# A routed expert layer on one core: the search's counts divided anew between VectorE and ScalarE

## The chip, the core and the metric

The kernel runs on one core of one Trainium2 chip. The metric is the time of one execution on the device in microseconds (us). It is measured several times; the median is given. The profile belongs to one more execution of the same program.

The engines that matter here are TensorE (PE: matmuls; PEld: its weight loads), VectorE (DVE), ScalarE (ACT) and GpSimd (POOL). Each works through its own instructions in the order in which the program lists them, and waits on semaphores for the others. What stands behind a waiting instruction on the same engine waits too.

## The reference

Three layers follow each other. The input is x of shape 8 x 3072 x 256.

```python
X = fft(fft(x, axis=1), axis=2).real            # 24576 tokens x 256
h = X @ w_in;  g = elu(h);  y = g @ w_out       # 256 -> 2048 -> 256
logits = y @ w_gate                             # 24576 x 8 experts
order = argsort(-logits.flatten())              # all token-expert pairs, best first
for idx in order:                               # greedy, each expert takes at most N // E = 3072
    tok, e = idx // 8, idx % 8
    if assigned[tok] < 0 and counts[e] < cap: assigned[tok] = e; counts[e] += 1
for e in range(8):                              # each expert: relu MLP 256 -> 1024 -> 256 on its tokens
    out[mask_e] = relu(y[mask_e] @ w1[e]) @ w2[e]
```

## The kernel before, in words

`moe1` (the first 1990 us) computes the transform and the first MLP and leaves the rows y in DRAM and the logits L in SBUF. `moe2` does the routing and the eight experts. The change lies in `moe2` alone.

**Routing.** The greedy assignment is done as eight selections, `select(i)`. Each finds the next expert to be full and the value at which it is. The logits lie as sortable 32-bit keys, one half-word in `hm` (upper half, masked) and one in `kl`, with 128 partitions (16 tokens by 8 experts) of 1536 columns. `level` (line 280) searches one half of the key bit by bit, 16 levels from bit 15 to 0, and `select` calls it twice, first on `hm`, then on `vm`. So a selection has 32 levels, and seven selections after the first have 224. A level counts the keys that reach a candidate `cand`: ScalarE counts `NA` = 512 columns with a Sign activation and an accumulator (line 287, result `c2`), VectorE counts `ND` = 1024 columns with a compare and an accumulator (line 288, result `c1`). TensorE adds the counts over the partitions with two or three matmuls of 8 columns (`c1`, line 298; `c0` in the second search, line 300; `c2`, line 301). VectorE compares the sums with the capacity (line 303, flags in `jk`, largest flag in `ok`) and makes the next candidate (line 305). The flags of each level are added to `score` (lines 292 and 306), and after the 32 levels the expert with the largest score is taken (lines 328 on).

**Listing.** `listing(i)` turns the selection into a list of token numbers. For each of 12 chunks it makes one-hot blocks on VectorE: `oq` (lines 473, 474 and the scaling by the partition number `pcol` in line 476) and `oh` (line 481). One step later `place` multiplies them on TensorE (line 452, 16 matmuls). It also fetches the expert's weights and splits them into two parts (ScalarE, GpSimd). For i = 0 the scaling stands on ScalarE already (line 478), and GpSimd does line 474.

**Experts.** `expert(i)` works on 6 groups of 512 tokens. A group has two stages. In the first ("hps stage"), eight blocks f of six matmuls of 512 columns (line 555, tile `hps`, three buffers); after each block ScalarE makes `hh` (line 567) and VectorE makes `hl` (line 573), which frees the `hps` buffer. Then eight transposes (line 533) bring in the next group, with `yh` on ScalarE and `yl` on VectorE. In the second ("acc stage"), 32 steps of three matmuls of 256 columns (lines 596 to 598), and after each 16 of them ScalarE copies a result (`osb`, line 603).

**Who sets the order.** Selections and listings for later experts are woven into the matmuls of the present expert by a small planner that runs while the program is built. It keeps three model clocks (`ck.pe`, `ck.dve`, `ck.act`). `pe(c)` advances the first; `act(d)` and `dve(d)` put d behind the later of the engine's own clock and `ck.pe` + 200. A level charges `dve(DR)` with `DR` = 940 and `act(700)` and yields `after()`, the later of both clocks plus 80: the due time. Between the matmuls the expert yields; the planner then steps the listing, or else the selection, if its due time has passed on `ck.pe` and `ck.dve` is not more than a slack ahead. A step of the selection is allowed after every step of the acc stage (327 model units each), but in the hps stage only after the first matmul of a block f (217 units) and after its last (1302). Each `hh` charges `act(480)`, each `hl` `dve(610)`, each `osb` `act(500)`. The planner fixes the order only; on the chip TensorE waits at a level's matmul until the counts are there.

The first selection and the first listing come before any expert, with nothing beside them. The last ten groups (two-thirds of expert 6 and all of expert 7) run with all selections and listings done.

Of the kernel before, what the change touches and what calls it, by code (L numbers as in the profile page):

```python
# [11 lines left out]
BF16 = mybir.dt.bfloat16  # L12
I32 = mybir.dt.int32
U16 = mybir.dt.uint16
AF = mybir.ActivationFunctionType
OP = mybir.AluOpType
AX = mybir.AxisListType

B, S, D, F, E, FE = 8, 3072, 256, 2048, 8, 1024
# [142 lines left out]
def moe2(tc, yd, R, w1, w2, out):  # L162
    nc = tc.nc
# [4 lines left out]
    with ExitStack() as ctx:  # L168
        con = ctx.enter_context(tc.tile_pool(name="con2", bufs=1))
        ctx.enter_context(nc.allow_low_precision(reason="counts up to 2048 are exact in float16"))  # L170
        rt = ctx.enter_context(tc.tile_pool(name="rt", bufs=1))
# [6 lines left out]
        def rps(shape, dtype=F32):  # L178
            return psum.tile(shape, dtype, name="rps")

        pcol = con.tile([128, 1], F32, name="pcol")
# [12 lines left out]
        score = con.tile([128, E], F32, name="score")  # L194
# [25 lines left out]

        setup = consts()
        NT = NC * 128
        ND = 1024
        NA = NT - ND

        def small(name, w=1, dtype=F32, bufs=2):
            return rt.tile([128, w], dtype, name=name, bufs=bufs)
# [7 lines left out]
        now = [-1]  # L235
        draining = [False]
        WAIT = 10000
        SW, S1, S2, AF0, DR, PM, FR = 1000, 1300, 2000, 80, 940, 1, 2

        class Clock:  # L240
            pe = dve = act = ready = 0
# [6 lines left out]
        def act(d):  # L248
            ck.act = max(ck.act, ck.pe + 200) + d

        def dve(d, after=0):
            ck.dve = max(ck.dve, ck.pe + 200, after) + d
# [3 lines left out]
        def after():  # L256
            return max(ck.dve, ck.act) + AF0

        def select(i):
            if i:  # L260
# [8 lines left out]
                for hf in range(2):  # L269
# [7 lines left out]
                    dve(900)  # L277
                    yield after()

            def level(src, c0=None):  # L280
                cand = small("cand")
                nc.vector.memset(cand, 32767.5)
                thr = float(2 * CAP - 16 * (NA + (NT if c0 is not None else 0)))
                for k in range(15, -1, -1):
                    w = float(1 << k)
                    c1, c2, low = small("c1", 1, F16), small("c2", 1, F16), small("low")
                    nc.scalar.activation(junk2[:, 0:NA], src[:, ND:], AF.Sign, bias=cand, scale=-1.0, accum_out=c2)
                    nc.vector.tensor_scalar(junk[:, 0:ND], src[:, 0:ND], cand, None, op0=OP.is_ge, op1=OP.add,  # L288
                                            accum_out=c1)
                    nc.vector.tensor_scalar(low, cand, 0.5 - w if k == 0 else -w / 2, None, op0=OP.add)  # L290
                    if k < 15:
                        nc.vector.tensor_tensor(score, score, jk, op=OP.add)
                    next(setup, None)
                    dve(DR)
                    act(700)
                    yield after()
                    ps = rps([128, E])
                    nc.tensor.matmul(ps, c1.to_broadcast([128, 128]), es2, start=True, stop=False)
                    if c0 is not None:
                        nc.tensor.matmul(ps, c0.to_broadcast([128, 128]), esn, start=False, stop=False)  # L300
                    nc.tensor.matmul(ps, c2.to_broadcast([128, 128]), esn, start=False, stop=True)
                    ok, jk = small("ok"), small("jk", E)
                    nc.vector.tensor_scalar(jk, ps, thr, None, op0=OP.is_ge, op1=OP.max, accum_out=ok)
                    cand = small("cand")
                    nc.vector.scalar_tensor_tensor(cand, ok, w, low, op0=OP.mult, op1=OP.add)
                nc.vector.tensor_tensor(score, score, jk, op=OP.add)
                return cand

            nc.vector.memset(score, 0.0)
            hi = yield from level(hm)  # L310
            c0, hib = small("c0", 1, F16), small("hib")
            nc.vector.tensor_scalar(hib, hi, 0.5, None, op0=OP.add)
# [9 lines left out]
            nc.vector.tensor_scalar(gm, hm, hi, None, op0=OP.is_ge)  # L322
            dve(600)
            lo = yield from level(vm, c0)
            smx, sv, mn, sel = small("smx"), small("sv", E), small("mn"), small("sel", E)
            key, sgn, th, wix = (small(n, 1, I32) for n in ("key", "sgn", "th", "wix"))
            wb = rt.tile([128, 16], BF16, name="wb")
            nc.vector.tensor_reduce(smx, score, op=OP.max, axis=AX.X)
            nc.vector.tensor_copy(key, lo)
            nc.vector.scalar_tensor_tensor(sv, score, smx, em8, op0=OP.is_equal, op1=OP.mult)  # L330
# [82 lines left out]
        def listing(i):  # L413
# [35 lines left out]
            def place(c, oh, oq):  # L449
                pl = rps([128, 48]) if i else pl0  # L450
                for j in range(16):
                    nc.tensor.matmul(pl, oh[:, :, j], oq[:, :, j], start=j == 0 and (i > 0 or c == 0),  # L452
                                     stop=j == 15 and (i > 0 or c == NC - 1))
                if i == 0:
                    return
                if c:
                    nc.vector.tensor_tensor(pj, pl, pj, op=OP.add)
                else:
                    nc.vector.tensor_copy(pj, pl)

            for c in range(NC):
                js = slice(16 * c, 16 * c + 16)
                if i:
                    oh = rt.tile([128, 128, 16], BF16, name="oh", bufs=2)
                    oq = rt.tile([128, 48, 16], BF16, name="oq", bufs=2)
                else:
                    oh = ex.tile([128, 128, 16], BF16, name=("yh", "yl")[c % 2])
                    oq = ex.tile([128, 48, 16], BF16, name="h%s%d" % ("hl"[c % 2], c // 2), bufs=1)

                def row(a, n):  # L470
                    return a[:, js].unsqueeze(1).to_broadcast([128, n, 16])

                nc.vector.tensor_tensor(oq[:, 24:48], io16[:, 0:24], row(qb, 24), op=OP.is_equal)
                (nc.vector if i > 0 else nc.gpsimd).tensor_tensor(oq[:, 0:24], oq[:, 24:48], row(jb, 24), op=OP.mult)
                if i > 0:
                    nc.vector.tensor_scalar(oq[:, 24:48], oq[:, 24:48], pcol, None, op0=OP.mult)
                else:
                    nc.scalar.activation(oq[:, 24:48], oq[:, 24:48], AF.Copy, scale=pcol)
                dve(900)
                yield 0  # L480
                nc.vector.tensor_tensor(oh, io16, row(rb, 128), op=OP.is_equal)
                if prev:
                    place(*prev)
                prev = (c, oh, oq)
                dve(1300)
                if ck.pe > fetched + WAIT:
                    next(parts, None)
                yield after()
# [128 lines left out]
        class Stream:  # L617
# [9 lines left out]
            def step(self):  # L627
# [6 lines left out]
                return False  # L634

        sel_s = Stream(select, E)
        lst_s = Stream(listing, E)

        def ready(i):
# [655 lines left out]
```

## Time and profile before

| | us |
|---|---|
| median of 3 runs (3556.1 to 3559.21) | 3558.7 |
| the profiled execution | 3554.52 |
| its span, first to last instruction | 3552.7 |
| TensorE busy | 3348.4 (94%) |
| VectorE busy | 2784.1 (78%) |
| ScalarE busy | 2139.5 (60%) |
| GpSimd busy | 650.7 (18%) |
| mean granted clock of TensorE | 0.974 |

The busy share is an average over stages with different limits: until 1985 us TensorE is busy without a break, from 1997.3 to 2110 us it is nearly idle, then it shares its time between experts and routing, and from 3308.6 us on it has the experts alone. What a change of the routing is worth is read from the second and third stage.

### The profile page before, as it was taken

How to read it: one execution, taken by the hardware profiler on the slowest of the kernel's cores; microseconds unless marked ns; L12 is line 12 of the kernel's file. 1: busy time of each engine (PE TensorE's matmuls, PEld its weight loads, DVE VectorE, ACT ScalarE, POOL GpSimd, SP SyncE). 2: the span in 40 equal slices, each digit the busy share in tenths (PEclk: the TensorE clock that was granted, in tenths of full speed). 3: DMA queues.
4: the chain of work that ended last, by engine and by line, in shares of the span. 5: the costliest groups of instructions: out<-in, count | busy, mean ns of one | idle time of the engine just before them, and what ended most of it. 6: DMA issues, size and time to landing. Idle time of an engine off the chain costs nothing.

```text
span 3552.7 us, 62569 instructions
## 1 busy us (share of the span) xinstructions
PE 3348.4 (94%) x25464; PEld 3111.3 (88%) x25464; DVE 2784.1 (78%) x5264; ACT 2139.5 (60%) x2945; POOL 650.7 (18%) x836
## 2 busy tenths in 40 slices
PE   7999999999999999999999549999999999999998
PEld 4999999999999999999999437878788887888997
DVE  7888888888888888788778888787878788887332
ACT  4777777778777777787777534343434344343232
POOL 4000000000000000000000053333333342424232
PEclk9999999999999999999999759999999999999999
DMA  7112121121121211211100011111111011111110
GB/s 197 31 51 46 43 41 46 36 45 35 42 45 44 41 46 36 45 35 42 32 13 13 13 41 39 54 58 33 60 36 60 28 60 34 60 37 59 39 48 30
DMA packets 97080, 159.31 MB, mean 45 GB/s; under 512 B 18464, under 2 KB 68632, under 8 KB 94616
## 3 DMA queue, kind: packets, MB, share of 16 engines
q1 hardware_dynamic: 67016, 64.05, 7.5%
q0 software_dynamic: 24576, 80.21, 7.2%
q10 hardware_dynamic: 5200, 11.05, 1.0%
q8 instruction: 200, 3.28, 0.4%
q14 instruction: 88, 0.72, 0.1%
HBM read 91.78 MB, written 63.47 MB: 44 GB/s over the span
## 4 chain that ended last, share of the span: by engine, by line
PE 79%; DVE 17%; issue 1%; DMA 1%; ACT 0%; POOL 0%; SPq 0%; DVEq 0%; POOLq 0%; ACTq 0%
PE acc L1115 10%; PE acc L1114 10%; PE acc L1116 10%; PE hps L555 10%; DVE junk L288 7%; PE pq L1061 5%; PE pq L1063 5%; PE pq L1062 5%; PE acc L596 4%; PE acc L598 3%; PE acc L597 3%; PE rps L452 3%; PE pq L1065 3%; DVE hl L573 2%; PE pq L788 2%
## 5 line engine op out<-in xcount | busy, mean ns | idle before, releaser
L1116 PE MATMUL acc<-woh,gl 128*128 128x264 f32 x3072 | 872.8, 284 | 1.4 <-DVE gl L1101 1.4
L1115 PE MATMUL acc<-wol,gh 128*128 128x264 f32 x3072 | 874.1, 285 | 0.0
L1114 PE MATMUL acc<-woh,gh 128*128 128x264 f32 x3072 | 873.0, 284 | 1.0 <-DVE wol L1035 1.0
L1116 PEld LDWEIGHTS acc<-woh,gl 128*128 128x128 f32 x3072 | 578.0, 188 | 2.0 <-DVE gl L1101 1.9
L1114 PEld LDWEIGHTS acc<-woh,gh 128*128 128x128 f32 x3072 | 578.5, 188 | 1.2 <-issue 1.2
L1115 PEld LDWEIGHTS acc<-wol,gh 128*128 128x128 f32 x3072 | 577.6, 188 | 0.0
L1084 ACT ACTIVATE e<-h 128x1024 f32<-128x1024 f32 x384 | 407.8, 1062 | 158.9 <-DVE h L1078 158.9
L1077 DVE TENSOR_TENSOR h<-pq,qs 128x512 f32<-128x512 f32 x384 | 265.5, 691 | 283.3 <-ACT qs L1071 282.3
L1101 DVE TENSOR_TENSOR gl<-g,gh 128x1024 fp32r<-128x1024 f32 x384 | 468.5, 1220 | 1.5 <-ACT gh L1096 1.5
L1091 DVE SCALAR_TENSOR_TENSOR g<-e,h 128x1024 f32<-128x1024 f32 x384 | 467.3, 1217 | 0.1
L596 PE MATMUL acc<-w2h,hh 128*128 128x256 f32 x1536 | 453.3, 295 | 0.0
L598 PE MATMUL acc<-w2h,hl 128*128 128x256 f32 x1536 | 434.9, 283 | 7.5 <-DVE hl L573 7.5
L597 PE MATMUL acc<-w2l,hh 128*128 128x256 f32 x1536 | 435.2, 283 | 0.0
L573 DVE SCALAR_TENSOR_TENSOR hl<-hps,hh 128x512 fp32r<-128x512 f32 x384 | 259.3, 687 | 221.1 <-ACT hh L567 213.4
L1086 ACT ACTIVATE e<-e 128x1024 f32<-128x1024 f32 x384 | 407.3, 1061 | 10.7
L1096 ACT ACTIVATE gh<-g 128x1024 fp32r<-128x1024 f32 x384 | 403.7, 1051 | 2.1 <-PE acc L1115 2.1
L567 ACT ACTIVATE hh<-hps 128x512 fp32r<-128x512 f32 x384 | 227.9, 595 | 283.2 <-PE hps L555 238.4
L1071 ACT ACTIVATE qs<-pq 128x512 f32<-128x512 f32 x384 | 229.4, 597 | 208.7 <-PE pq L1065 204.2
L606 POOL DMA_INDIRECT out<-osb,yg x192 | 201.2, 1048 | 734.6 <-ACT osb L603 705.3
L555 PE MATMUL hps<-yh,w1h 128*128 128x512 f32 x768 | 311.1, 405 | 15.8 <-DVE hl L573 14.9
L555 PE MATMUL hps<-yh,w1l 128*128 128x512 f32 x768 | 309.4, 403 | 0.0
L555 PE MATMUL hps<-yl,w1h 128*128 128x512 f32 x768 | 304.9, 397 | 0.0
(320 smaller groups left out, 7525.4 us busy)
## 6 DMA issues: line engine op xcount, KB each, us to landing
yd<-ysb SPq DMA_DIRECT2D x48, 514.0 KB
zd<-zev SPq DMA_DIRECT2D x30, 385.5 KB
xa<-x SPq DMA_DIRECT2D x28, 384.0 KB
zt<-zd SPq DMA_DIRECT2D x16, 193.5 KB
xa<-w_out ACTq DMA_DIRECT2D x6, 512.0 KB
zt<-zd SPq DMA_DIRECT2D x32, 96.0 KB
yg<-yd,idx POOLq DMA_INDIRECT x192
out<-osb,yg POOLq DMA_INDIRECT x192
```

The costliest lines, as they stand in the source:

```text
L555: nc.tensor.matmul(ps, w[:, ws], v[:, c], start=c + k == 0, stop=c + k == 3)
L596: nc.tensor.matmul(acc[t // 2][:, t % 2], hh[:, ts], w2h[:, fs], start=f == 0, stop=False)
L597: nc.tensor.matmul(acc[t // 2][:, t % 2], hh[:, ts], w2l[:, fs], start=False, stop=False)
L598: nc.tensor.matmul(acc[t // 2][:, t % 2], hl[:, ts], w2h[:, fs], start=False, stop=f == 7)
L1084: nc.scalar.activation(e, st["h"], AF.Relu, scale=-1.0)
L1086: nc.scalar.activation(st["e"], st["e"], AF.Exp, scale=-1.0)
L1091: nc.vector.scalar_tensor_tensor(g, st["e"], -1.0, st["h"], op0=OP.add, op1=OP.max)
L1096: nc.scalar.activation(st["gh"], st["g"], AF.Copy)
L1101: nc.vector.tensor_tensor(st["gl"], st["g"], st["gh"], op=OP.subtract)
L1114: nc.tensor.matmul(o, st["gh"][:, i, ts], woh(c), start=c == 0, stop=False)
L1115: nc.tensor.matmul(o, st["gh"][:, i, ts], wol(c), start=False, stop=False)
L1116: nc.tensor.matmul(o, st["gl"][:, i, ts], woh(c), start=False, stop=c == 15)
```

## The change

- A level divides its 1536 columns differently: in selections 1 to 7 VectorE counts 640 and ScalarE 896 (before: 1024 and 512), in selection 0 VectorE counts 832 and ScalarE 704.
- The flags of a level are no longer added to `score` at once. Line 303 writes them into a slot of a new tile `hist` (128 x 32 x 8, bf16), and one reduction over the 32 slots gives `score` at the end of a selection. 30 additions in the loop, two behind it, and the clearing of `score` are gone.
- In listings 1 to 7 the scaling of the one-hot block by `pcol` stands on ScalarE, as it did for listing 0.
- The planner's charges are changed to go with it: a level charges `dve(750)` and `act(1000)`, the first half of a listing chunk `dve(750)` and `act(450)` (before: `dve(900)` alone).

```diff
-        ND = 1024
-        NA = NT - ND
...
-        SW, S1, S2, AF0, DR, PM, FR = 1000, 1300, 2000, 80, 940, 1, 2
+        SW, S1, S2, AF0, PM, FR = 1000, 1300, 2000, 80, 1, 2
...
+            ND = 640 if i else 832
+            NA = NT - ND
+            hist = rt.tile([128, 32, E], BF16, name="hist")
+
             def level(src, c0=None):
...
                     nc.vector.tensor_scalar(low, cand, 0.5 - w if k == 0 else -w / 2, None, op0=OP.add)
-                    if k < 15:
-                        nc.vector.tensor_tensor(score, score, jk, op=OP.add)
                     next(setup, None)
-                    dve(DR)
-                    act(700)
+                    dve(750)
+                    act(1000)
                     yield after()
...
-                    ok, jk = small("ok"), small("jk", E)
-                    nc.vector.tensor_scalar(jk, ps, thr, None, op0=OP.is_ge, op1=OP.max, accum_out=ok)
+                    ok = small("ok")
+                    nc.vector.tensor_scalar(hist[:, k + 16 * (c0 is not None)], ps, thr, None, op0=OP.is_ge,
+                                            op1=OP.max, accum_out=ok)
...
-                nc.vector.tensor_tensor(score, score, jk, op=OP.add)
                 return cand
 
-            nc.vector.memset(score, 0.0)
...
+            nc.vector.tensor_reduce(score, hist.rearrange("p k e -> p e k"), op=OP.add, axis=AX.X)
             nc.vector.tensor_reduce(smx, score, op=OP.max, axis=AX.X)
...
-                if i > 0:
-                    nc.vector.tensor_scalar(oq[:, 24:48], oq[:, 24:48], pcol, None, op0=OP.mult)
-                else:
-                    nc.scalar.activation(oq[:, 24:48], oq[:, 24:48], AF.Copy, scale=pcol)
-                dve(900)
+                nc.scalar.activation(oq[:, 24:48], oq[:, 24:48], AF.Copy, scale=pcol)
+                dve(750)
+                act(450)
                 yield 0
```

## Rows read from the trace of the kernel before

**Rows 1.** Page: span, busy time by engine, the chain's shares by line.
```profile
span 3552.7 us, 62569 instructions
...
PE 3348.4 (94%) x25464; PEld 3111.3 (88%) x25464; DVE 2784.1 (78%) x5264; ACT 2139.5 (60%) x2945; POOL 650.7 (18%) x836
...
PE acc L1115 10%; PE acc L1114 10%; PE acc L1116 10%; PE hps L555 10%; DVE junk L288 7%; PE pq L1061 5%; PE pq L1063 5%; PE pq L1062 5%; PE acc L596 4%; PE acc L598 3%; PE acc L597 3%; PE rps L452 3%; PE pq L1065 3%; DVE hl L573 2%; PE pq L788 2%
```

**Rows 2.** Busy time by window: length, then us (x instructions) per engine.
```profile
core 0: us, PE busy (x) PEld busy (x) DVE busy (x) ACT busy (x) POOL busy (x), PEclk, DMA share, GB/s
1997.30:2067.00 69.70, 7.32 (x80) 4.67 (x81) 60.96 (x249) 27.79 (x66) 0.00 (x0) 0.50 0.02 5
...
2150.20:2163.80 13.60, 12.39 (x59) 8.90 (x59) 12.38 (x41) 8.77 (x18) 6.28 (x8) 1.00 0.20 59
2163.80:2178.80 15.00, 14.06 (x124) 13.07 (x123) 13.32 (x47) 7.34 (x16) 2.17 (x4) 1.00 0.05 19
...
3331.70:3342.70 11.00, 11.00 (x51) 9.07 (x50) 4.84 (x7) 4.78 (x8) 4.95 (x7) 1.00 0.16 49
3342.70:3354.90 12.20, 12.20 (x105) 12.20 (x104) 1.92 (x2) 2.22 (x3) 3.12 (x6) 1.00 0.14 44
```

**Rows 3.** Weight loads by line, 2112 to 3308.6: busy, mean, idle before, releasers.
```profile
L598 PEld LDWEIGHTS acc<-w2h,hl 128*128 128x128 f32 x1216 | 232.9, 192 | 8.4 <-DVE hl L573 8.4
...
L555 PEld LDWEIGHTS hps<-yh,w1h 128*128 128x128 f32 x609 | 116.8, 192 | 42.6 <-DVE hl L573 20.5 <-issue 1.3
...
L298 PEld LDWEIGHTS <-c 128*128 128x128 f16 x224 | 21.5, 96 | 104.7 <-DVE junk L288 83.2 <-issue 14.1 <-DVE score L292 5.0
```

**Rows 4.** Durations by line (ns min/median/max, first and last start, shapes).
```profile
L288 DVE TENSOR_SCALAR_CACHE_REDUCE junk<-hm,cand x128: 1278/1279/1282, 1997.4 to 3172.8; 128x1024 bf16<-128x1024 uint16 x128
L287 ACT ACTIVATE junk<-hm,cand x128: 712/722/725, 1997.8 to 3172.8; 128x512 bf16<-128x512 uint16 x128
L313 ACT ACTIVATE junk<-hm,hib x8: 1575/1576/1577, 2031.4 to 3175.0; 128x1536 bf16<-128x1536 uint16 x8
L328 DVE TENSOR_REDUCE smx<-score x8: 161/161/161, 2067.3 to 3216.1; 128x1 f32<-128x8 f32 x8
L262 DVE TENSOR_REDUCE m<-L x7: 1737/1742/1747, 2109.8 to 3080.4; 128x192 f32<-128x1536 f32 x7
L476 DVE TENSOR_SCALAR oq<-oq,pcol x84: 319/321/3173, 2215.3 to 3298.4; 128x384 bf16<-128x384 bf16 x84
L478 ACT ACTIVATE hh<-hh,pcol x6: 614/616/617, 2075.8 to 2100.3; 128x384 bf16<-128x384 bf16 x6
```

**Rows 5.** Timeline of one level of the first selection (start us, us, engine, line).
```profile
2027.05 1.28 DVE L288 TENSOR_SCALAR_CACHE_REDUCE junk<-hm,cand 128x1024 bf16<-128x1024 uint16 x1
...
2028.39 0.10 PEld L298 LDWEIGHTS <-c 128*128 128x128 f16 x1 [1.94 <-DVE junk L288]
...
2028.41 0.12 PEld L301 LDWEIGHTS <-c 128*128 128x128 f16 x1
...
2028.65 0.17 DVE L303 TENSOR_SCALAR_CACHE_REDUCE jk<-rps 128x8 f32<-128x8 f32 x1 [0.17 <-PE rps L301]
...
2029.12 1.28 DVE L288 TENSOR_SCALAR_CACHE_REDUCE junk<-hm,cand 128x1024 bf16<-128x1024 uint16 x1
2029.21 0.72 ACT L287 ACTIVATE junk<-hm,cand 128x512 bf16<-128x512 uint16 x1 [1.26 <-DVE cand L305]
2029.83 0.19 ACT L287 ACTIVATION_READ_ACCUMULATOR junk<-hm,cand 128x1 f16 x1
```

**Rows 6.** Timeline: two successive levels in an acc stage, twelve matmuls between them.
```profile
2487.46 0.10 PEld L298 LDWEIGHTS <-c 128*128 128x128 f16 x1 [0.52 <-DVE junk L288]
...
2489.52 0.10 PEld L298 LDWEIGHTS <-c 128*128 128x128 f16 x1 [0.53 <-DVE junk L288]
```

**Rows 7.** Timeline of VectorE in an hps stage, between two counts.
```profile
2656.18 0.68 DVE L573 SCALAR_TENSOR_TENSOR hl<-hps,hh 128x512 fp32r<-128x512 f32 x1
2656.78 0.16 DVE L303 TENSOR_SCALAR_CACHE_REDUCE jk<-rps 128x8 f32<-128x8 f32 x1
```

## The prediction

> **What bounds the kernel now.** I began with the page. TensorE is busy for 94% of the span, yet the chain that ended last has the count on VectorE, line 288, among its larger lines with 7%, more than any single expert line of the second part but one [rows 1]. So there is a stage in which a count on VectorE sets the pace although VectorE is not the busiest engine.
>
> Then the windows [rows 2]. In the first selection (1997.3 to 2067 us) TensorE does 7.3 of 69.7 us, and VectorE is busy for 61: this stretch is nothing but levels, one behind the other. In the experts I set a group with a selection beside it against one without. Without, the hps stage takes 11.0 us and the acc stage 12.2, and TensorE has no gap. With a selection they take 13.6 and 15.0, together 5.4 us more. The group with a selection holds 183 TensorE instructions against 156; the 27 more are ten levels of two or three small matmuls.
>
> Third, what TensorE waits for from 2112 to 3308.6 us. Its weight loads in line 298, the first small matmul of a level, are preceded by 104.7 us of idle time over 224 levels, 0.47 each; the count on VectorE ends 83.2 of it. Waits for `hl` in lines 555 and 598 are 20.5 and 8.4 us [rows 3]. These 134 us are about what a faster routing can give back in the experts; the last ten groups have nothing to give.
>
> **The level, part by part.** Read one level of the first selection [rows 5]. VectorE's count starts at 2027.05, TensorE loads the sum of `c1` at 2028.39 (1.34 later) and that of `c2` at 2028.41 (1.36 later), the flags follow at 2028.65 and the next count at 2029.12. ScalarE starts 0.09 us after VectorE and its accumulator is read out 0.62 + 0.19 us later, so its count is there 0.90 us after VectorE's start. VectorE is last by 0.4 us: that is the slack which the new division spends.
>
> The prices. ScalarE takes 722 ns for 512 columns and 1576 for 1536, so 0.834 ns a column: 882 ns for 704, 1042 for 896 [rows 4]. For VectorE's count there is one width, 1279 ns for 1024. Its slope I bound by two rows: a VectorE reduction takes 161 ns for 8 elements and 1742 for 1536, 1.035 ns a column, and the count can't fall faster than in proportion, 1.249 ns. I take 1.035, since it comes from an instruction of the same engine that also runs through all columns and gives one number: 640 columns 0.40 us less (up to 0.48), 832 columns 0.20 us less (up to 0.24).
>
> *Selection 0* (832 and 704). VectorE's leg falls to 1.14 us. ScalarE's rises to 0.90 + 0.16 = 1.06, and some 0.06 to reach TensorE, the delay that stands between the end of VectorE's count and the load. The two are level, and a level gains 0.20 us: 32 x 0.20 = 6.4. The additions to `score` in the loop stand where VectorE waits for TensorE anyway (idle 0.17 before the flags [rows 5]): nothing. At the end two additions of about 0.1 fall away. The reduction of 256 elements costs 161 + 248 x 1.035 = 418 ns; its stride of eight elements is shown in no row, so between 0.4 and, at twice that, 0.8. Sum: 6.4 + 0.2 - 0.4 = 6.2 us, all on the path.
>
> *Selections 1 to 7* (640 and 896). VectorE's leg falls to 0.94, but ScalarE's rises to 0.90 + 0.32 = 1.22, with the hand-over 1.28 against the 1.36 at which `c2` was loaded. So of the 0.40 us only 0.08 come out of the loop; in the second search one more small matmul (line 300) moves ahead of the wait, for which I add up to 0.04. I take 0.10: the loop of 2.06 us between two successive levels of an acc stage [rows 6] becomes 1.96.
>
> That alone would be 22 us. The rest hangs on the planner's order, which I work out from its charges. In the **acc stage** a level was due 200 + 940 + 80 = 1220 units after it was placed, and is now due after 200 + 1000 + 80 = 1280. Steps of 327 let it in at 1308 in both cases: twelve matmuls between two levels, as in rows 6. They are worth 1.44 us (12.2 us less the transposes over 32 steps, 0.36 a step), the loop needs 2.06, the small matmuls 0.09, and the wait is 0.53. It becomes 0.43. Where an `osb` falls between, the new due time slips to five steps, and the wait nearly goes (0.07).
>
> In the **hps stage** ScalarE's clock carries `hh` as well. Before: 200 + 480 + 700 + 80 = 1460 units, and the next opening is at 1519, seven matmuls on. At 11.0 / 48 = 0.23 us these are worth 1.6 us, while the loop has an `hl` in it, behind which the flags stand on VectorE (0.60 us from the start of the one to the other [rows 7]). So TensorE waits here too. After: 200 + 480 + 1000 + 80 = 1760 misses that opening, and the next is at 2604: twelve matmuls or 2.75 us. The loop with an `hl` needs 1.96 + 0.60 = 2.56. The wait should go.
>
> Carrying the three clocks through one steady group I get four levels in the hps stage (after blocks 0, 2, 4 and 6) and seven in the acc stage (after steps 5, 10, 14, 18, 23, 27 and 31). That is eleven, so the selection does not fall behind (ten in the group of rows 2). Waits of a group: 4 x 0.43, 2 x 0.07, about 0.3 after step 5, where VectorE is still at `yl`, and 0.25 from step 31 to the end of block 0 (one step and six matmuls, 1.73 us): 2.4 us. 224 levels are 20.4 such groups: 49 us of waits in place of 104.7, **56 us** less. By the stages of rows 2: excess 5.4 us for ten levels now, 2.4 + 11 x 0.09 = 3.4 for eleven then, times 224 levels: 121 less 69, **52 us**. I take 50, a little under both, since the first levels of a selection meet the end of a listing and not a steady group.
>
> The seven reductions stand between the last level and the matmuls of line 342. If TensorE waits for each, they cost 7 x 0.42 = 2.9 us; I charge all of it.
>
> **The listing.** VectorE loses 84 instructions of 321 ns, 27 us; ScalarE takes them at 616 ns [rows 4], 52 us, beside 224 x 0.32 = 72 us of longer counts. GpSimd and the DMA queues issue what they did. The new wait is ScalarE's for line 474 on VectorE, and behind it on ScalarE stand `hh` and `osb`, for which `hl` and TensorE wait. From above: each scaling delays TensorE by its full 0.62 us, 52 lost. From below: all waits for `hl` in rows 3 go, 29 gained. I take 0: the block is used by TensorE one chunk later, and three `hps` buffers let `hh` come late by a block or two. If that cover is gone, it is the third rival below.
>
> **The sum.** 3554.5 (the profiled execution) - 6.2 - 50 + 2.9 = 3501.2. The median stands 4.2 above the profiled execution, so I forecast **3505**, and 3485 to 3525 if only the sizes are off.
>
> **The rivals.**
> 1. *Only the shorter loop.* The longer count lies in front of `hh` on ScalarE (0.32 us), `hl` follows late, and the wider spacing in the hps stage is used up by it. Then 22 + 6.2 - 2.9 = 25 us: 3533. For it: 2.75 against 2.56 is a thin margin. Against: ScalarE has room there, 8.8 busy of 13.6 us [rows 2].
> 2. *Hidden.* A wait taken from line 298 shows up at the next instruction of TensorE, and only the first selection gains: 3558.7 - 6.2 + 2.9 = 3555. Against it: in the groups without a selection TensorE has no gap at all.
> 3. *ScalarE becomes the bound, slower.* Scalings (52) and the longer counts in hps stages (four in eleven of 224, 81 x 0.32 = 26) hold `hh` by 78 us, against 53 gained: 3505 + 78 = 3583. It decides once two thirds of these holds reach TensorE, which needs `hh` to be late by more than the buffers bear, some 2.75 us. For it: VectorE is sometimes late by that much; one scaling took 3173 ns [rows 4]. Against: in the usual chunk 0.6 us stand against that cover.
> The Trainium skill ("ScalarE: Activation LUTs", section Rules for kernel authors) speaks for the third: multiplications belong on VectorE, not on ScalarE. The trace agrees on the price of one, 321 against 616 ns. By the rule the move costs 84 x 0.295 = 25 us (3530) wherever engine time is the bound; by the rows it is not, for ScalarE is idle for a third of such a stage now [rows 2].
> 4. *More.* Waits for `hl` go as well, since VectorE is freer: another 29 us, 3476.
>
> **How the numbers follow.** Forecast 0.62, the first rival 0.14, the second 0.06, the third 0.07, the fourth 0.11. For 8 in 10 the range takes in the first rival's and the fourth's centre and leaves out the second and third: 3474 to 3546. A measurement of this kernel can tell about 0.2% (7 us) from no change. Faster: 0.62 + 0.14 + 0.11 = 0.87; same 0.06; slower 0.07.
>
> **What would show it.** In the profile after: line 288 at about 0.88 us for 640 and 1.08 for 832 columns, line 287 at 1.04 and 0.88; a first selection of some 63.5 us; in the experts twelve hps matmuls between levels instead of six or seven, with no idle time in front of line 298 or 301 there; about 0.43 us in the acc stages, now in front of line 301, with ScalarE as releaser; the sum of both lines near 50 us. A hps stage with a selection near 11.6 us and an acc stage near 15. What would make the forecast wrong: waits of line 555 for `hl` well above 20 us, or ScalarE's `hh` waiting behind line 478.

## The result and the profile after

| | before | after |
|---|---|---|
| median, same chip, 4 runs each (us) | 3557.7 (3556.1 to 3559.2) | 3498.8 (3497.0 to 3501.2) |
| profiled execution | 3554.5 | 3501.2 |
| span | 3552.7 | 3499.4 |

The ratio is 0.984 [0.982, 0.985]: the change saves 59 us by the medians and 53.3 us between the two profiled executions. The forecast was 3505, and 3501.2 for the profiled execution. The total was met; several of its terms were not, and their errors cancelled.

Page after, to be read against [rows 1]: span, busy time by engine, shares of the chain that ended last.

```profile
span 3499.4 us, 62303 instructions
...
PE 3343.9 (96%) x25464; PEld 3121.6 (89%) x25464; DVE 2637.1 (75%) x4924; ACT 2253.9 (64%) x3029; POOL 649.7 (19%) x836
...
PE hps L553 14%; PE acc L1113 11%; PE acc L1112 11%; PE acc L1114 11%; PE pq L1059 5%; PE pq L1061 5%; PE pq L1060 5%; PE acc L594 4%; PE acc L595 4%; PE acc L596 4%; PE rps L452 3%; PE pq L1063 3%; ACT junk L289 3%; PE pq L786 2%; PE pq L865 1%
```

VectorE's count has left the chain, where it held 7%. ScalarE's count (line 289 now) stands in it with 3%: it is the new last leg of a level. TensorE's own lines took over the rest; `hps` alone rose from 10% to 14%.

Windows after, with the columns of [rows 2]: the first selection, then two groups with a selection beside them (hps stage, acc stage, hps stage, acc stage).

```profile
2000.00:2064.00 64.00, 7.35 (x80) 4.70 (x81) 53.16 (x218) 32.94 (x66) 0.00 (x0) 0.50 0.02 5
2147.40:2158.90 11.50, 11.50 (x58) 8.87 (x57) 9.85 (x32) 9.05 (x17) 5.84 (x7) 1.00 0.19 56
2158.90:2173.10 14.20, 13.86 (x120) 13.10 (x119) 10.63 (x41) 8.72 (x15) 2.30 (x6) 1.00 0.09 29
2173.10:2184.80 11.70, 11.70 (x63) 9.02 (x62) 9.74 (x31) 9.43 (x17) 5.96 (x8) 1.00 0.19 57
2184.80:2200.00 15.20, 14.64 (x127) 13.51 (x126) 10.47 (x44) 9.23 (x17) 2.18 (x4) 1.00 0.08 27
```

The first selection, from its first count to the maximum over the scores, shrank from 69.9 to 64.0 us. A hps stage takes 11.5 or 11.7 instead of 13.6 us, and in both TensorE is busy from end to end. The two acc stages take 14.2 and 15.2 us against 15.0, with five and seven levels in them against six: there some idle time is left (0.3 and 0.6 us here).

Weight loads after, 2105 to 3260 us, with the columns of [rows 3]: busy, mean, idle before, releasers.

```profile
L596 PEld LDWEIGHTS acc<-w2h,hl 128*128 128x128 f32 x1216 | 233.9, 192 | 0.2 <-DVE hl L571 0.2
...
L553 PEld LDWEIGHTS hps<-yh,w1h 128*128 128x128 f32 x624 | 118.8, 190 | 24.5 <-DVE hl L571 5.1
...
L531 PEld LDWEIGHTS tps<-identf,yg 128*128 128x128 f32 x317 | 38.3, 146 | 23.5 <-DMA yg<-yd,idx 18.3 <-issue 0.2
L301 PEld LDWEIGHTS <-c 128*128 128x128 f16 x224 | 21.9, 98 | 19.4 <-ACT junk L289 18.9
L298 PEld LDWEIGHTS <-c 128*128 128x128 f16 x224 | 21.7, 97 | 42.3 <-issue 17.3 <-DVE junk L290 7.8 <-DVE low L292 6.3
...
L342 PEld LDWEIGHTS <-gm 128*128 128x128 bf16 x84 | 3.0, 96 | 3.0 <-issue 2.7
```

The third and the last of these lines have counterparts in the kernel before that [rows 3] didn't hold (2105 to 3308.6 us):

```profile
L533 PEld LDWEIGHTS tps<-identf,yg 128*128 128x128 f32 x312 | 36.1, 144 | 11.5 <-DMA yg<-yd,idx 8.2 <-issue 0.2
...
L342 PEld LDWEIGHTS <-gm 128*128 128x128 bf16 x84 | 2.6, 96 | 1.2 <-issue 1.0
```

So the ledger of TensorE's waits in the experts reads: in front of a level's matmuls 104.7 -> 19.4 + 42.3 = 61.7 (-43.0); for `hl` 28.9 -> 5.3 (-23.6); for the token rows that the transposes need 8.2 -> 18.3 (+10.1). That is -56.5. VectorE spends 4.3 us on the seven reductions (0.61 us each), but TensorE waits only 1.8 us more for the matmuls of line 342 behind them (1.2 -> 3.0): -54.7. From the first to the last matmul of `hps` the experts took 1409.7 us before (2117.8 to 3527.5) and 1359.8 after (2114.4 to 3474.2): **-49.9**. The first expert matmul starts 3.4 us earlier: -6.0 from routing (5.9 of them in the first selection), +2.6 in the first 1990 us, whose code is unchanged. The tail is 25.2 us in both. -49.9 - 3.4 = -53.3, the difference of the spans.

### The profile page after: what moved, and what is told of

Its sections match the earlier page's. It is cut to its first block, busy times and chain, and to the rows that moved or that the text cites. A ratio compares the mean times of both kernels' runs of the same rounds, so it can differ in the third digit from the quotient of the medians.

```text
span 3499.4 us, 62303 instructions
## 1 busy us (share of the span) xinstructions
PE 3343.9 (96%) x25464; PEld 3121.6 (89%) x25464; DVE 2637.1 (75%) x4924; ACT 2253.9 (64%) x3029; POOL 649.7 (19%) x836
## 4 chain that ended last, share of the span: by engine, by line
PE 85%; DVE 6%; ACT 4%; issue 2%; DMA 1%; POOL 0%; another core or an unknown queue 0%; ACTq 0%; DVEq 0%; POOLq 0%
PE hps L553 14%; PE acc L1113 11%; PE acc L1112 11%; PE acc L1114 11%; PE pq L1059 5%; PE pq L1061 5%; PE pq L1060 5%; PE acc L594 4%; PE acc L595 4%; PE acc L596 4%; PE rps L452 3%; PE pq L1063 3%; ACT junk L289 3%; PE pq L786 2%; PE pq L865 1%
```

## What was tested

The theory that I took to the chip ("order"): the gain comes from the planner's new charges, which put twelve matmuls instead of six or seven between two levels of a hps stage; without them the shorter loop gives little. The rival ("work"): VectorE's shorter leg and fewer instructions give the gain by themselves, whatever the order.

All medians of one batch come from one chip and stand against the kernel before there (3543.3, 3547.2 and 3556.1 us). Waits are sums of TensorE's weight loads in the experts, in us; "length" is first to last `hps` matmul. `c_first_only` changes nothing in the experts, so it gives the values of the unchanged experts for its batch. Two executions of one kernel differ here: `b_old_charges` and `b_again` are one kernel, and so are `e_split832` and `e_again`, and their lengths are 5.0 and 11.8 us apart (last section). A few us between two rows say little unless the trace shows where they come from.

| kernel | batch | median | ratio [95%] | levels | `hl` | fetch | length |
|---|---|---|---|---|---|---|---|
| c_first_only | 1 | 3542.1 | 0.9993 [0.9982, 1.0004] | 100.6 | 26.6 | 2.6 | 1396.3 |
| a_charges_only | 1 | 3514.3 | 0.9912 [0.9894, 0.9929] | 74.8 | 11.6 | 19.1 | 1366.7 |
| b_old_charges | 1 | 3490.3 | 0.9847 [0.9830, 0.9865] | 62.2 | 11.2 | 2.5 | 1349.4 |
| d_scale_vector | 1 | 3493.9 | 0.9857 [0.9840, 0.9874] | 53.3 | 4.4 | 16.9 | 1352.8 |
| z_after (the change) | 2 | 3485.3 | 0.9822 [0.9805, 0.9840] | 53.1 | 5.4 | 14.5 | 1344.4 |
| b_again | 2 | 3492.8 | 0.9835 [0.9815, 0.9854] | 61.9 | 13.3 | 8.1 | 1354.4 |
| e_split832 | 2 | 3478.5 | 0.9801 [0.9784, 0.9818] | 51.8 | 5.7 | 12.5 | 1337.4 |
| h_act850 | 2 | 3489.4 | 0.9828 [0.9810, 0.9846] | 58.2 | 4.5 | 14.8 | 1350.0 |
| e_again | 3 | 3489.1 | 0.9811 [0.9792, 0.9830] | 60.3 | 5.7 | 14.2 | 1349.2 |
| k_early_lists | 3 | 3474.8 | 0.9770 [0.9752, 0.9787] | 59.3 | 8.4 | 4.4 | 1333.0 |
| j_old_split832 | 3 | 3497.6 | 0.9830 [0.9812, 0.9849] | 72.2 | 11.8 | 4.5 | 1361.2 |
| f_no_hist | 3 | 3497.4 | 0.9831 [0.9812, 0.9850] | 62.6 | 6.0 | 18.4 | 1356.4 |

### The order alone

```diff
 # kernel before, with only the new charges
-                    dve(DR)
-                    act(700)
+                    dve(750)
+                    act(1000)
...
-                dve(900)
+                dve(750)
+                act(450)
                 yield 0
```

> The kernel before with the planner's new charges alone (a level dve(750), act(1000); the first half of a listing chunk dve(750), act(450)); all the work stays as it was, 1024 columns on VectorE and 512 on ScalarE, the scaling on VectorE. Theory of the order (mine): most of the gain is the wider spacing of levels in the hps stages, which follows from the charges and not from the work. Then twelve hps matmuls (2.75 us) stand between levels, the loop with an hl in it needs 2.06 + 0.60 = 2.66, and the wait goes there; in the acc stages the wait stays at 0.53 per twelve matmuls. Waits in front of line 298 fall from 104.7 to some 65 us: 3518 us. Theory of the work (rival): VectorE's relief is what counts and the order follows it; then the time stays within 10 us of before, 3548 to 3560.

Measured: 29 us less, about half of the change's gain, where "order" wanted most of it. Weight loads of this kernel (2105 to 3300 us):

```profile
L556 PEld LDWEIGHTS hps<-yh,w1h 128*128 128x128 f32 x638 | 121.2, 190 | 25.9 <-DVE hl L574 6.2
L534 PEld LDWEIGHTS tps<-identf,yg 128*128 128x128 f32 x320 | 38.6, 146 | 24.0 <-DMA yg<-yd,idx 19.1 <-issue 0.2
L298 PEld LDWEIGHTS <-c 128*128 128x128 f16 x224 | 21.6, 96 | 74.6 <-DVE junk L288 55.1 <-DVE hl L574 14.1 <-issue 2.1
```

Spacing takes 26 us off the waits of line 298 and 15 off those for `hl`. With 1024 columns VectorE's count is still the last leg (55.1 us). The longer fetch wait is here too, with none of the work moved: it belongs to the order. The eight executions with the new charges have 12.5 to 19.1 us of it, the five with the old charges 2.5 to 8.2.

### The work alone

```diff
 # kernel after, with the old charges
-                    dve(750)
-                    act(1000)
+                    dve(940)
+                    act(700)
...
-                dve(750)
-                act(450)
+                dve(900)
                 yield 0
```

> The changed kernel with the old charges (a level dve(940), act(700); the first half of a chunk dve(900)): the work is moved, the order stays. Theory of the order: the first selection gains 6, the loop is 0.10 us shorter (22 us), and in the hps stages, where six or seven matmuls still stand between levels, a wait is left since hh comes behind the longer count on ScalarE: 3525 to 3535 us. Theory of the work: nearly the whole gain, 3495 to 3508 us.

> The kernel with the work moved and the old charges once more, now beside the changed one. Theory that spacing and work are two ways to one and the same gain: the two kernels differ by little, and what differs is the fetch of the next expert's rows (waits of the transposes: none here, 10 to 20 us there); then this one is 5 to 15 us faster than the changed kernel. Theory that the new charges add their own 29 us: this one is 20 us or more slower.

Measured: 53 us less without any wider spacing. "Order" wanted 3525 to 3535 and falls. Repeated beside the whole change (`z_after`) it came out 7.5 us above it, where I had now expected it below; the spreads of the two (3486.5 to 3495.7 and 3483.7 to 3487.9) just overlap. So the order adds little to the work, and no loss shows. The timeline of `b_again` shows why six matmuls are enough (VectorE and ScalarE in a hps stage):

```profile
2178.42 0.88 DVE L290 TENSOR_SCALAR_CACHE_REDUCE junk<-vm,cand 128x640 bf16<-128x640 uint16 x1
2178.48 1.04 ACT L289 ACTIVATE junk<-vm,cand 128x896 bf16<-128x896 uint16 x1
...
2179.29 0.68 DVE L570 SCALAR_TENSOR_TENSOR hl<-hps,hh 128x512 fp32r<-128x512 f32 x1
2179.43 0.19 ACT L289 ACTIVATION_READ_ACCUMULATOR junk<-vm,cand 128x1 f16 x1
...
2179.55 0.10 PEld L298 LDWEIGHTS <-c 128*128 128x128 f16 x1 [0.28 <-DVE low L292]
...
2179.89 0.17 DVE L303 TENSOR_SCALAR_CACHE_REDUCE hist<-rps 128x8 bf16<-128x8 f32 x1
...
2180.30 0.88 DVE L290 TENSOR_SCALAR_CACHE_REDUCE junk<-vm,cand 128x640 bf16<-128x640 uint16 x1
```

VectorE ends its 640 columns 0.9 us after it began and goes on to `hl`, while ScalarE still counts; when TensorE has both counts added, VectorE has nearly finished `hl`. The loop takes 1.88 us with an `hl` in it, and I had 1.96 + 0.60. In the kernel before, three counts of VectorE in a hps stage with an `hl` between each two:

```profile
2654.84 1.28 DVE L288 TENSOR_SCALAR_CACHE_REDUCE junk<-hm,cand 128x1024 bf16<-128x1024 uint16 x1
...
2657.17 1.28 DVE L288 TENSOR_SCALAR_CACHE_REDUCE junk<-hm,cand 128x1024 bf16<-128x1024 uint16 x1
...
2659.51 1.28 DVE L288 TENSOR_SCALAR_CACHE_REDUCE junk<-hm,cand 128x1024 bf16<-128x1024 uint16 x1
```

2.33 us. So the work takes 0.45 us off this level with an `hl`, and 0.09 off one without (below). It is so throughout: between two levels with seven `hps` matmuls (35 times) the median falls from 2.14 to 1.79 us, with six (20 times) from 2.34 to 1.81, with twelve matmuls of the acc stage (62 times) from 2.07 to 1.95. Summed up from `c_first_only` to `b_old_charges`, which have the same order, the intervals of six and seven give 27 of the 47 us that the experts gain, those of twelve 14.

### Is it the columns that hide `hl`?

```diff
 # j_old_split832: the work alone, divided less far
-            ND = 640 if i else 832
+            ND = 832
```

> The work moved and the old charges, with 832 columns on VectorE and 704 on ScalarE. In this order six or seven hps matmuls stand between levels. Theory that at 640 an hl is hidden there beside ScalarE's longer count: at 832 VectorE's count ends only when ScalarE's does, the hl comes behind it, and the intervals of six and seven matmuls grow from 1.9 to some 2.1, while those of twelve matmuls in the acc stage shrink from 1.96 to 1.87; the two cancel, within 5 us of b_again, 0.983 of before. Rival, that only the later of the two legs counts: intervals of 1.87 everywhere, 8 to 12 us faster than b_again, 0.980.

Measured 0.9830, level with `b_again`'s 0.9835, as the theory of the hidden `hl` has it. The two stand in different batches; the intervals show it more surely. With 832 columns two levels of the acc stage with twelve matmuls between them come quicker (median 1.86 us instead of 1.95), those of a hps stage slower: 1.89 instead of 1.79 with seven matmuls between them and 2.06 instead of 1.81 with six, where the rival had 1.87 everywhere. Line 298 waits for VectorE again (2105 to 3300 us), first here, then in `b_again`:

```profile
L301 PEld LDWEIGHTS <-c 128*128 128x128 f16 x224 | 21.9, 98 | 0.0
L298 PEld LDWEIGHTS <-c 128*128 128x128 f16 x224 | 21.5, 96 | 72.2 <-DVE low L292 28.1 <-DVE junk L290 24.9 <-issue 10.7
```

```profile
L301 PEld LDWEIGHTS <-c 128*128 128x128 f16 x224 | 21.6, 97 | 22.2 <-ACT junk L289 19.0
L298 PEld LDWEIGHTS <-c 128*128 128x128 f16 x224 | 21.5, 96 | 39.7 <-DVE low L292 17.5 <-issue 11.5 <-DVE junk L290 1.4
```

### The even division with the new order

```diff
 # e_split832 and e_again: the change, but
-            ND = 640 if i else 832
+            ND = 832
```

> The changed kernel with 832 columns on VectorE and 704 on ScalarE in all selections, charges as changed. Both legs of a level are then about level (1.14 and 1.12) and the loop 1.87 in place of 1.96. If the loop is all that the acc stages wait for: 75 intervals of twelve matmuls by 0.09 less, 7 us faster than the changed kernel. If VectorE's relief counts (0.20 us more work of VectorE in 224 levels, an hl no longer fits beside ScalarE's count): 5 to 20 us slower than it.

> The changed kernel with 832 and 704 columns in all selections, once more, beside the next three on one chip: 0.980 of before. The transposes wait some 10 us for the fetched rows.

Measured 6.8 us less than the change on the same chip, with no overlap of the runs: the size that was expected, but not for the reason given. The 75 intervals of twelve matmuls in the acc stages, which were to give it, take 139.0 us in `z_after` and 139.9 in `e_split832`. The waits of line 301 for ScalarE are gone (20.0 to 0.3 us), but those of line 298 rise from 33.1 to 51.5. What gets shorter is the way from an acc stage into a hps stage: the 14 intervals of three acc and six `hps` matmuls take 26.5 us in place of 30.4. Where the order gives a level twelve matmuls in the hps stage, `hl` no longer needs hiding there, and the even division does a little better. `e_again` gave 0.9811 in the next batch, where its old-charge twin `j_old_split832` was 8.5 us slower, again without overlap. So the new charges are worth some 8 us on top of the work (7.5 and 8.5 side by side), not 29: **the two halves of the change are two ways to the same waits.**

### The list that comes late

With the new charges the transposes for expert 2 stand still. Timeline after, TensorE's loads and GpSimd's fetches:

```profile
2458.23 0.97 POOL L522 DMA_INDIRECT yg<-yd,idx  x1 [14.99 <-issue]
...
2461.01 0.29 PEld L531 LDWEIGHTS tps<-identf,yg 128*128 128x128 f32 x2 [4.40 <-DMA yg<-yd,idx]
2462.32 0.29 PEld L531 LDWEIGHTS tps<-identf,yg 128*128 128x128 f32 x2 [1.02 <-DMA yg<-yd,idx]
2464.78 0.72 PEld L531 LDWEIGHTS tps<-identf,yg 128*128 128x128 f32 x4 [2.17 <-DMA yg<-yd,idx]
```

The fetches are issued 3 us ahead of their use, 1.25 us apart; in the kernel before, the like fetches begin at 2460.94 and their transposes at 2477.51, 16.6 us later. The selections have become longer, measured in TensorE's matmuls: selections 1 and 2 took 2.7 and 2.5 groups (48 `hps` and 96 acc matmuls each) from first level to last, and take 3.0 and 3.0 now. The second, whose list expert 2 needs, ends 104 matmuls (0.7 of a group) later. The clock falls with it:

```profile
2456.00:2481.20 25.20, 17.77 (x128) 15.54 (x127) 9.81 (x42) 8.33 (x14) 9.87 (x13) 0.80 0.19 53
```

The granted clock of this stretch is 0.80 in the mean: part of it ran at 1.2 and not at 2.4 GHz. In steps of 5 us from 2455 on the clock is 0.76, 0.50, 0.72, 1.00 and 1.00, so it fell during the 7.6 us of waits for rows and rose behind them. Two kernels ask what would bring the list earlier: a smaller charge on ScalarE's clock, or the old order for the first two selections in the experts.

```diff
 # h_act850: the change, but
-                    act(1000)
+                    act(850)
```

> The changed kernel with a level charged act(850) in place of act(1000). The due time in the hps stage, 1610, still misses the opening at 1519, so twelve matmuls stay between levels there; in the acc stages it slips to five steps less often, so a selection takes fewer groups and the next list is ready earlier. Theory that the longer due time delays the list: the waits of the transposes fall from 10 to 20 us to below 5, while the acc stages wait a little more; 5 to 12 us faster than the changed kernel. Rival, that these waits come from the listing's own charges: no change, within 4 us.

Missed: 3489.4 against 3485.3, too near to tell apart, and the fetch wait stands at 14.8 us. In selections 1 and 2, on which the first lists depend, a level comes at the same place as with 1000 or one step of the acc stage earlier: in the hps stage both due times, 1610 and 1760, fall between the same two openings, 1519 and 2604.

```diff
 # k_early_lists: the even division, and the old order for selections 1 and 2
-            ND = 640 if i else 832
+            ND = 640 if i in (1, 2) else 832
...
-                    dve(750)
-                    act(1000)
+                    dve(940 if i in (1, 2) else 750)
+                    act(700 if i in (1, 2) else 1000)
```

> As e_again, but selections 1 and 2 with the old level charges (940, 700) and 640 columns on VectorE, selections 3 to 7 with the new charges and 832. Theory that the wait for the fetched rows comes from the first lists, which the new charges end a quarter of a group later: the waits of the transposes fall from 10 us to below 2, the granted clock stays up there, and the kernel is 6 to 12 us faster than e_again. Rival, that they come from the listing's charges, which stay as in e_again: no change, within 4 us.

Measured 14.3 us less than `e_again` beside it, more than expected, and the lowest ratio of all: 0.977 [0.975, 0.979]. Weight loads, 2105 to 3300 us, and the window 2430 to 2480 us, of `e_again`:

```profile
L531 PEld LDWEIGHTS tps<-identf,yg 128*128 128x128 f32 x326 | 38.5, 143 | 19.3 <-DMA yg<-yd,idx 14.2
```

```profile
2430.00:2480.00 50.00, 42.94 (x289) 36.85 (x288) 27.86 (x80) 18.72 (x36) 14.78 (x19) 0.90 0.12 35
```

and the same of `k_early_lists`:

```profile
L531 PEld LDWEIGHTS tps<-identf,yg 128*128 128x128 f32 x334 | 39.5, 144 | 9.0 <-DMA yg<-yd,idx 4.4 <-issue 0.2
```

```profile
2430.00:2480.00 50.00, 46.72 (x317) 40.27 (x316) 36.04 (x116) 27.11 (x52) 17.79 (x24) 0.97 0.14 44
```

The fetch wait falls by 9.8 us and the clock stays up: the wait does come from the late list. But the 14.3 us are not the price of that list. Counted from the first matmul of expert 0, expert 2 begins only 3.5 us earlier than in `e_again`, since the old order had put the kernel 6.0 us behind before the fetch. And `e_again` loses 8.7 us in experts 2 and 3 at two levels with long waits that `e_split832`, the same kernel, does not have (last section). Against `e_split832` the experts of `k_early_lists` are 4.4 us shorter. That early lists are worth more than this is not shown.

### The smaller parts

```diff
 # c_first_only: kernel before, but
-        ND = 1024
+            ND = 1024 if i else 832
```

> The kernel before with 832 columns on VectorE and 704 on ScalarE in selection 0 alone. The first selection is 32 x 0.20 = 6.4 us shorter, nothing else moves: 3551 us. If ScalarE's leg were the later one by more than I think, half of it: 3554.

The time can't tell it (0.9993, with 1 inside the interval). By the trace the first selection takes 63.6 us for 69.9 in the kernel before, measured from the first count to the maximum over the scores: -6.3, where 32 x 0.20 = 6.4 was forecast for the division alone.

```diff
 # d_scale_vector: the change, but the scaling of listings 1 to 7 on VectorE with its old charges
-                nc.scalar.activation(oq[:, 24:48], oq[:, 24:48], AF.Copy, scale=pcol)
-                dve(750)
-                act(450)
+                if i > 0:
+                    nc.vector.tensor_scalar(oq[:, 24:48], oq[:, 24:48], pcol, None, op0=OP.mult)
...
+                dve(900)
```

> The changed kernel with the scaling of listings 1 to 7 back on VectorE and its charge dve(900) without act(450). My forecast gave the move nothing: 3499 us, within 5. If the waits for hl that fell from 28.9 to 5.3 us between the two traces fell because VectorE is rid of 84 scalings, they come back here: 3510 to 3522. If ScalarE's waits at line 475 (126 us in all) hold TensorE, it is faster here: below 3490.

0.9857, against 0.984 and 0.9822 for the change in the result and in batch 2; with the first the intervals overlap, with the second they touch. If the move to ScalarE is worth anything it is a gain of up to some 12 us (0.35% of 3547), and not the loss that a price of 616 for 321 ns suggests. The waits for `hl` do not come back (4.4 us), so it is not the move of the scaling that took them away. Which wait it takes away I can't show: the waits of this kernel differ from the change's by less than two executions of one program do.

```diff
 # f_no_hist: the change, but the flags are added in the loop again
+                    if k < 15:
+                        nc.vector.tensor_tensor(score, score, jk, op=OP.add)
...
-            nc.vector.tensor_reduce(score, hist.rearrange("p k e -> p e k"), op=OP.add, axis=AX.X)
```

> The changed kernel with the flags added to score in every level, as before, and without the reduction. If the additions lie where VectorE waits anyway and the reduction (0.608 us, eight times) lies on the path: 5 us faster than the changed kernel. If in the hps stages the addition stands in front of an hl or the flags: 224 x 0.08 at most, 18 us slower, and the reduction given back, some 5 us: between 5 us faster and 13 slower; near 0.982 of before if both cancel.

0.9831, against 0.984 and 0.9822 for the change: no difference that can be told. TensorE's wait in front of the matmuls behind the selection is 1.2 us again, as before the change. Summing the flags once is neither a gain nor a loss of a size that shows. That the additions stood in VectorE's waiting time fits this; no run shows it by itself.

> The changed kernel itself, beside the next three on one chip. Both theories: 0.984 of before. Its waits: some 57 us in front of the level's matmuls, some 5 for hl, some 10 to 20 in front of the transposes for the fetch of the next expert's rows.

The change in batch 2: 0.982, at the lower end of the result's interval.

## Why the prediction came out, point by point

**Prices: right.** Durations after (ns min/median/max, starts, shapes), to be read against [rows 4]:

```profile
L290 DVE TENSOR_SCALAR_CACHE_REDUCE junk<-hm,cand x128: 878/879/1080, 2000.0 to 3158.3; 128x640 bf16<-128x640 uint16 x112, 128x832 bf16<-128x832 uint16 x16
...
L289 ACT ACTIVATE junk<-hm,cand x128: 882/1042/1045, 2000.3 to 3158.4; 128x896 bf16<-128x896 uint16 x112, 128x704 bf16<-128x704 uint16 x16
...
L327 DVE TENSOR_REDUCE score<-hist x8: 595/608/620, 2063.3 to 3204.8; 128x8 f32<-128x256 bf16 x8
...
L475 ACT ACTIVATE oq<-oq,pcol x84: 604/617/621, 2219.1 to 3271.6; 128x384 bf16<-128x384 bf16 x84
```

879 and 1080 ns were forecast as 0.88 and 1.08 us, 1042 and 882 as 1.04 and 0.88: a slope borrowed from another instruction of the engine held. The reduction was mis-sized: 608 ns instead of 418, within the bounds (0.4 to 0.8), so seven take 4.3 instead of 2.9 us on VectorE; TensorE's waits for them grew by 1.8 us.

**First selection: right.** 64.0 us against some 63.5; by the same marks 5.9 us less than before, where 6.2 was forecast.

**The loop of an acc stage: right in size.** Two successive levels after, with [rows 6] as their counterpart:

```profile
2170.05 0.10 PEld L298 LDWEIGHTS <-c 128*128 128x128 f16 x1
...
2170.37 0.10 PEld L301 LDWEIGHTS <-c 128*128 128x128 f16 x1 [0.21 <-ACT junk L289]
...
2172.34 0.10 PEld L301 LDWEIGHTS <-c 128*128 128x128 f16 x1 [0.21 <-ACT junk L289]
```

1.97 us from one to the next, forecast 1.96, and ScalarE is the releaser; the median of 75 such intervals is 1.94. The gap booked in front of line 301 is 0.21, not 0.43, because TensorE already does the matmuls of `c1` and `c0` in that time; twelve matmuls of 0.12 us still leave some 0.4 us beyond the levels' own matmuls.

**The order: right.** Two levels of a hps stage after, twelve matmuls apart, with nothing but an issue gap in front of each:

```profile
2174.57 0.10 PEld L298 LDWEIGHTS <-c 128*128 128x128 f16 x1 [0.27 <-issue]
...
2177.49 0.10 PEld L298 LDWEIGHTS <-c 128*128 128x128 f16 x1 [0.26 <-issue]
```

2.92 us, which is also the median of 55 such intervals. From 2174 to 2200 us the four levels of the hps stage and the seven of the acc stage stand where the clocks carried through put them.

**The reason given for the gain: half wrong.** The failed step is "The loop with an `hl` needs 1.96 + 0.60". `hl` runs beside ScalarE's longer count, and a loop with it takes 1.88 us in `b_again`. Even in the kernel before, it added 2.33 - 2.06 = 0.27 and not 0.60. The 0.60 ran from the start of `hl` to the flags, but without an `hl` the flags wait for TensorE at that place: 0.26 us from the load to the flags in [rows 5]. The sum counted that time twice. From the 0.60 it followed that without the wider spacing only the first rival's 25 us would be left; the work alone gave 53.

**Waits for `hl`: the size was off.** I left them at 28.9 us; they fell to 5.3, and that is the mechanism of the fourth rival (its 3476 was not reached). Each half of the change does it: 11.6 with the order alone, 11.2 with the work alone.

**"The selection does not fall behind": failed.** Eleven levels per group came about, but the ten that I set against them were no measure. The group of [rows 2] holds the break between the two searches of a selection, in which no level stands for 8.1 us. Over whole selections 1 and 2 the kernel before took 2.7 and 2.5 groups, and the kernel after 3.0. So the selections do fall behind, and the list for expert 2 came about when its rows were needed; I never set the end of a list against the fetch that waits for it. Price: 10 us of waits.

**The level waits: too low, 49 against 61.7.** In another execution of the same program (`z_after`) they were 53.1; the difference sits in three long waits of the result's execution, described in the last section.

**The sum.** Forecast for the experts -50 + 2.9 = -47.1, measured -49.9. Against the forecast stand -23.6 for `hl`, +10.1 for late rows, +7.0 for the level waits (-43 where I took -50) and -1.1 for the reductions (1.8 where I charged 2.9). Together -54.7; the 4.8 us up to -49.9 are not assigned. So the total was met because errors of both signs met in it: that part is luck.

**The rivals.** The first (only 25 us) is wrong even for the kernel with old spacing. The second (hidden) falls: TensorE's next instructions did not wait in place of the levels; only the 10.1 us for late rows came back. The third (ScalarE the bound) falls by its own sign: waits for `hl` fell. ScalarE does wait for VectorE at the scaling, as I feared (waits of ScalarE, 2100 to 3260 us: total, times, longest):

```profile
ACT oq L475 <- DVE oq L474: 126.0, 66, 4.9
```

but little of this reached TensorE, whose waits for `hl` are 5.3 us. The Trainium skill's rule for that rival ("ScalarE: Activation LUTs", section Rules for kernel authors: multiplications belong on VectorE) gave 3530. The kernel with the multiplication on VectorE should then be some 25 us (0.7%) faster than the change; at 0.9857 against 0.984 and 0.9822 it is not. The measurement decides.

## What to carry to other kernels

When two engines each have a leg of a latency loop and one of them has other work to fit into it, give that one the shorter leg: its other work then runs while the second leg ends (1.88 us with an `hl` inside, against 2.33). Where the steps of the loop stand further apart there is nothing to hide, and the even division did better by 6.8 us. Two edits that attack the same waits don't add (29 and 53 gave about 60), so price each alone and both together. A wider spacing can make a background job longer though its steps wait less (here 3.0 groups in place of 2.5 to 2.7): set the end of the job against its first user before you count the gain.

## What the runs showed of the hardware that I had not expected

VectorE's count with an accumulator costs 1.04 ns a column over three widths (879, 1080 and 1279 ns at 640, 832 and 1024) plus 0.21 us. The reduction over a stride of eight elements took 608 ns for 256 elements, where 161 + 248 x 1.035 = 418 had been the estimate.

One program differed by 15 us between two batches (1359.8 us in the experts of the result's profile, 1344.4 in `z_after`). The chip alone does not explain such differences: the kernel before came to 3543.3 and to 3556.1 us in batches 1 and 3 on one chip. The order of the instructions is the same in the two executions, so their levels can be set against each other one by one. 13.8 us of the difference lie in three places: 3.9 from 2132 to 2139 us, 4.1 from 2645 to 2648, 5.8 from 2806 to 2813. Each holds a long wait in front of line 298 (1.8, 2.9 and 3.7 us) and a stretch at the lower clock (windows after, columns of [rows 2]; the last is the first of the three places):

```profile
2645.00:2652.00 7.00, 6.71 (x44) 6.41 (x45) 4.00 (x21) 4.15 (x9) 1.06 (x2) 0.76 0.01 2
2804.00:2810.00 6.00, 3.50 (x18) 3.33 (x19) 2.75 (x14) 2.27 (x4) 0.00 (x0) 0.65 0.06 22
2135.00:2142.00 7.00, 5.77 (x37) 5.55 (x38) 4.22 (x20) 4.07 (x8) 0.35 (x1) 0.76 0.00 0
```

The longest of them, with the matmul whose sum VectorE needs there:

```profile
2801.15 0.17 PE L301 MATMUL rps<-esn,c 128*128 128x8 f16 x1
...
2804.94 0.17 DVE L303 TENSOR_SCALAR_CACHE_REDUCE hist<-rps 128x8 bf16<-128x8 f32 x1 [4.10 <-remote]
```

VectorE had nothing to do from 2800.8 us on, and the profile names no instruction that released it. `e_again` has long waits at the same three levels, `e_split832`, the same kernel, has none there. What held the engines is open; no run was made for it. The kernel before has long waits of its own in the result's profile: its experts took 1409.7 us there, and 1396.3, unchanged, in `c_first_only`. So the ratio hardly moves: 0.984 in the result, 0.982 in batch 2.
